# Feeding the first token tiles of a linear-attention kernel by transposing DMAs in place of TensorE transposes

## The chip, the cores and the metric

The kernel runs on one core of a Trainium2 chip. The metric is the device time of one execution in microseconds (us). Before the change it is 194.15 us, the median of three runs (194.1 to 194.21). The profiles are each of one profiled execution of the same program.

## What is computed

Two linear-attention blocks, A and B, read the same input x (2048 tokens, 640 features, bf16), each with its own weights, and a gate mixes them. Cut to what matters:

```python
g = sigmoid((x * gate_w).sum(-1, keepdims=True))
def block(x, wqkv, wo):                 # 32 heads of 20 features
    q, k, v = split(x @ wqkv)
    phi = lambda t: where(t > 0, t + 1, exp(t)) + 1e-6
    kv = einsum("bhsd,bhse->bhde", phi(k), v);  z = phi(k).sum(tokens)
    return ((phi(q) @ kv) / (phi(q) . z + 1e-6)) @ wo
out = g * block(x, A_wqkv, A_wo) + (1 - g) * block(x, B_wqkv, B_wo)
```

## The kernel before

The 2048 tokens are 16 tiles of 128 (`NT`), the 640 features are 5 chunks of 128 (`NC`), and four tiles make a block of 512 tokens (`NB` is 4). In on-chip memory, `XN` holds x with tokens on the partitions and `XT` holds x turned, with features on the partitions. `WKA` and `WKB` hold the K weights, `WQA` and `WQB` the Q weights.

The work runs in stages. First comes K: for each tile, phi(K) = phi(x Wk) is made for A and for B. For one tile this is five pairs of matmuls, one pair for each chunk (512 and 128 columns), which add up in two PSUM banks; then ScalarE takes the exponential and VectorE does two passes. Four PSUM pairs go round. The order of the K stage is A tiles 0 to 3, B tiles 0 to 3, A tiles 4 to 7, B tiles 4 to 7, and so on. Then come Q with the products of x and phi(K), the output weights and denominators, and the output tiles.

K needs the turned x. For tiles 4 to 15 it comes from 15 transposing DMAs (lines 388 to 397), one for each block of four tiles and each chunk, so each turns 512 rows by 128 columns. For tiles 0 to 3, TensorE turns it: `load_xn` brings each tile in by a plain DMA, and `turn` (line 423) multiplies the five chunks by an identity into two PSUM banks (line 431); VectorE copies three chunks and ScalarE two chunks from there into `XT` (lines 445 and 443). For these four tiles K is written out by hand with `ks` (line 824), which calls `k_part` (line 450) for single pairs of tile and chunk; a pair waits only for its own chunk of x and of the weights. All later tiles go through `k_tile` (line 467), whose matmuls wait for all five chunks of the tile. `fill` (line 416) issues matmuls on constants into a bank that is not read.

Every instruction, also the issue of a DMA, goes on the queue of the engine that is named, in the order of the program, and an engine works through its queue in order. An operation waits on semaphores for the last writers of what it reads and for the readers of what it overwrites. SP does nothing but issue DMAs. Its queue before the change is, in order: four plain loads of x (tiles 0 to 3, 160 KB each), chunk 4 of A's K weights, B's K weights (800 KB), the gate column, the 15 transposing DMAs, A's Q weights, three plain loads of x (tiles 4 to 15, 640 KB each), constants, and three more 800 KB weights. ACT's queue begins with chunks 0 to 3 of A's K weights, 160 KB each. The gate column (`gw`, lines 380 to 387) is read by the second group of matmuls of each B tile in `k_tile`.

Of the kernel before, what the change touches and what calls it, by code (L numbers as in the profile page):

```python
# [8 lines left out]
ACT = mybir.ActivationFunctionType  # L9
# [8 lines left out]
NC = 5  # L18
# [187 lines left out]
def bass_gated_mix__linear_attn_block__linear_attn_block__prompt_kernel(  # L206
# [18 lines left out]
    with ExitStack() as es:  # L225
        E = es.enter_context

        def sb(name, shape, dtype=dt.bfloat16):
            return E(nc.sbuf_tensor(name, shape, dtype))
# [5 lines left out]
        XT = sb("XT", [128, NC, S])  # L235
# [33 lines left out]
        def bank(i, lo, hi, p0=0, p1=128):  # L269
            o = 512 * (i % 2)  # L270
            return PP[i // 2][p0:p1, o + lo : o + hi]
# [4 lines left out]
        def new_sem(name):  # L276
            n_sem[0] += 1
            return E(nc.semaphore(name="d%d_%s" % (n_sem[0], name)))
# [3 lines left out]
        def dma(eng, name, o_ap, i_ap, reads=(), writes=(), transpose=False, noncontig=None):  # L282
            sem = new_sem(name)

            def fn(engobj):
                if noncontig is not None:
                    with nc.allow_non_contiguous_dma(reason=noncontig):
                        ins = engobj.dma_start(o_ap, i_ap, transpose=transpose)
                else:
                    ins = engobj.dma_start(o_ap, i_ap, transpose=transpose)  # L290
                return ins.then_inc(sem, 16)

            return sch.op(eng, fn, reads=reads, writes=writes, name=name, sem=sem, total=16)

        def mms(steps, reads=(), writes=(), name=""):


            def fn(pe):
                ins = None
                for o, l, r, st, sp, tp in steps:  # L300
                    ins = pe.matmul(o, l, r, start=st, stop=sp, tile_position=tp)  # L301
                return ins

            return sch.op("PE", fn, reads=reads, writes=writes, name=name)
# [5 lines left out]
        def act(fn, reads=(), writes=(), name=""):  # L310
            return sch.op("ACT", fn, reads=reads, writes=writes, name=name)

        def dve(fn, reads=(), writes=(), name=""):
            return sch.op("DVE", fn, reads=reads, writes=writes, name=name)
# [4 lines left out]
        xin = A_x[0]  # L319


        def load_xn(eng, t0, t1):
            dma(
                eng,
                "xn%d" % t0,
                XN[:, t0:t1, :],
                xin[128 * t0 : 128 * t1, :].rearrange("(t p) f -> p t f", p=128),
                writes=[("XN", t) for t in range(t0, t1)],
            )

        def load_w(eng, name, dst, src, key):
            dma(eng, name, dst[:, :, 0:D], src.rearrange("(c p) f -> p c f", p=128), writes=[key])
# [15 lines left out]
        def load_wk(eng, X, c0, c1):  # L348
            dma(
                eng,  # L350
                "wk%s%d" % (X, c0),
                WK[X][:, c0:c1, 0:D],
                wqkv[X][128 * c0 : 128 * c1, D : 2 * D].rearrange("(c p) f -> p c f", p=128),
                writes=[("WK", X, c) for c in range(c0, c1)],
            )
# [10 lines left out]
                fill=0.0,  # L366
            ),
            reads=[("ONE",)],
            writes=[("IDN",)],
# [2 lines left out]
            lambda e: e.activation(SG[:, 2, 0:1], nc.const_aps.tensor(1.0, (128, 1), dt.float32), ACT.Exp),  # L372
            writes=[("SGE", 0)],
        )
        for t in range(4):
            load_xn("SP", t, t + 1)
            load_wk("ACT", "A", t, t + 1)
        load_wk("SP", "A", 4, NC)
        load_wk("SP", "B", 0, NC)
        dma(  # L380
            "SP",
            "gw",
# [2 lines left out]
            writes=[("GW",)],  # L385
            noncontig="one column",
        )
        for b in range(1, NB):
            for c in range(NC):
                dma(  # L390
                    "SP",
                    "xt%d_%d" % (b, c),
                    XT[:, c, 512 * b : 512 * b + 512],
                    xin[512 * b : 512 * b + 512, 128 * c : 128 * c + 128],
                    writes=[("XT", t, c) for t in range(4 * b, 4 * b + 4)],
                    transpose=True,
                )
        load_w("SP", "wqA", WQ["A"], wqkv["A"][:, 0:D], ("WQ", "A"))
        for b in range(1, NB):
            load_xn("SP", 4 * b, 4 * b + 4)  # L400
        dma("SP", "cst", CB[:, :], cap, writes=[("CST",)])
# [14 lines left out]
        def fill(bk, n, w=512):  # L416
            mms(
                [(bank(bk, 0, w), C1[:, 0:128], C1[:, 0:w], True, True, None)] * n,
                writes=[("PS", bk)],
                name="fill",  # L420
            )

        def turn(t, b0):
            for cs, bk in (((0, 1, 2), b0), ((3, 4), b0 + 1)):
                n = len(cs)
                dst = bank(bk, 0, 64 * n).bitcast(dt.bfloat16)

                def tr(pe, dst=dst, cs=cs):
                    ins = None
                    for i, c in enumerate(cs):  # L430
                        ins = pe.transpose(  # L431
                            dst[:, 128 * i : 128 * i + 128],
                            XN[:, t, 128 * c : 128 * c + 128],
                            IDN[:, :],
                        )
                    return ins

                sch.op("PE", tr, reads=[("XN", t), ("IDN",)], writes=[("PS", bk)], name="tr%d" % t)
                o = XT[:, cs[0] : cs[0] + n, 128 * t : 128 * t + 128]
                i = dst.rearrange("p (c s) -> p c s", c=n)  # L440
                ks = [("XT", t, c) for c in cs]
                if n == 2:
                    act(lambda e, o=o, i=i: e.activation(o, i, ACT.Copy), reads=[("PS", bk)], writes=ks)
                else:
                    dve(lambda e, o=o, i=i: e.tensor_copy(o, i), reads=[("PS", bk)], writes=ks)  # L445
# [4 lines left out]
        def k_part(X, t, pp, cs, first, last):  # L450
            P = PP[pp]
            xs = slice(128 * t, 128 * t + 128)
            bks = [("PS", 2 * pp), ("PS", 2 * pp + 1)]
            for c in cs:
                l = XT[:, c, xs]
                st, sp = first and c == cs[0], last and c == cs[-1]
                mms(
                    [
                        (P[:, 0:512], l, WK[X][:, c, 0:512], st, sp, None),
                        (P[:, 512:D], l, WK[X][:, c, 512:D], st, sp, None),  # L460
                    ],
                    reads=[("XT", t, c), ("WK", X, c)],
                    writes=bks,
                    name="k%s%d" % (X, t),
                )
# [355 lines left out]
                )  # L821


        def ks(*units):
            for t, c in units:
                k_part("A", t, t, (c,), c == 0, c == NC - 1)

        fill(4, 12, 256)
        turn(0, 6)
        fill(4, 1)  # L830
        ks((0, 0))
        turn(1, 6)
        ks((0, 1), (1, 0), (1, 1))
        turn(2, 6)
        ks((0, 2), (1, 2), (2, 0), (2, 1), (2, 2))
        turn(3, 6)
        ks((0, 3), (0, 4))
        ks((1, 3), (1, 4), (2, 3), (2, 4))
        ks(*[(3, c) for c in range(NC)])
        for t in range(4):  # L840
            k_tile("A", t, True)
        for b in range(NB):
            for X in BR:
# [114 lines left out]
```

## Time and profile before

| What | Value |
|---|---|
| Median of the runs | 194.15 us |
| Span of the profiled execution, first to last instruction | 191.9 us |
| Median less span | 2.25 us |
| TensorE (PE) busy | 188.2 us, 98% |
| VectorE (DVE), ScalarE (ACT), GpSimd (POOL) busy | 124.3, 75.0, 44.5 us |
| Start of B tile 0's K on PE | 11.01 us |
| Start of A tile 4's K on PE | 16.47 us |
| Start of Q on PE | 49.11 us |

Times of single events are counted from the first instruction. In the timeline, a row is a run of like instructions: start, length, engine, line of the code, operation, and what is written from what; a "q" behind the engine means that its queue only issues (a DMA). The length of an issue is the time that the queue was held by it. "To landing" is the time from the start of the issue until the data and its semaphore were there. The chain of waits follows the work that ended last back in time, naming at each step what released it. [...]

### The profile page before, as it was taken

Reading aid. Unit: us, or ns where it says so; the run is one execution under the profiler, and the core shown is the slowest. Engines: PE = TensorE matmul, PEld = TensorE weight load, DVE = VectorE, ACT = ScalarE, POOL = GpSimd, SP = SyncE. Lnnn points to the kernel's source line nnn. Section 1 sums busy time; section 2 is a strip of 40 time slices with the busy share of each in tenths; the row PEclk is TensorE's granted clock in tenths of the full one; section 3 lists DMA queues with packets and bytes.
Section 4 is the critical chain, followed back from the end, with each engine's and each line's share of the span. In section 5 each row is a group of like instructions: output and inputs, shape, how many; then the busy total and the mean of one; then the engine's idle time right before and its main releaser. Section 6 shows DMA issues by size and latency. Waiting matters only on the chain.

```text
span 191.9 us, 3569 instructions
## 1 busy us (share of the span) xinstructions
PE 188.2 (98%) x1428; PEld 103.6 (54%) x1428; DVE 124.3 (65%) x211; ACT 75.0 (39%) x130; POOL 44.5 (23%) x36
## 2 busy tenths in 40 slices
PE   7999999999999999999999999999999999999994
PEld 4555555555454444445454557555557555555553
DVE  0298999998996765757676744890422856582544
ACT  3466565565642624444335332122123533223310
POOL 1000223253226566536547410000000000000000
PEclk9999999999999999999999999999999999999999
DMA  5967569993400000011000003038596011111214
GB/s 186 319 119 102 100 104 373 366 352 102 126 3 0 0 3 0 21 43 43 3 0 2 0 25 85 3 67 222 155 254 239 3 68 69 37 68 68 72 38 132
DMA packets 22785, 19.07 MB, mean 99 GB/s; under 512 B 10288, under 2 KB 22000, under 8 KB 22768
## 3 DMA queue, kind: packets, MB, share of 16 engines
q1 hardware_dynamic: 21904, 18.08, 33.4%
q10 hardware_dynamic: 864, 0.76, 1.2%
q8 instruction: 11, 0.18, 0.4%
q14 instruction: 6, 0.05, 0.1%
HBM read 12.94 MB, written 3.93 MB: 88 GB/s over the span
## 4 chain that ended last, share of the span: by engine, by line
PE 96%; DMA 1%; DVE 1%; issue 0%; DVEq 0%
PE ps L301 95%; DMA XN<-in_A_x_dram 1%; PE ps L431 1%; DVE OSTG L796 0%; DVE XT L445 0%; DVEq L928 0%; DVEq L158 0%
## 5 line engine op out<-in xcount | busy, mean ns | idle before, releaser
L525 ACT ACTIVATE EQ<-ps 128x512 bf16<-128x512 f32 x40 | 23.9, 597 | 34.1 <-PE ps L301 34.0
L484 ACT ACTIVATE EK<-ps 128x640 bf16<-128x640 f32 x32 | 22.3, 703 | 16.1 <-PE ps L301 15.2
L530 DVE TENSOR_SCALAR EQ<-EQ 128x512 bf16<-128x512 bf16 x40 | 15.3, 383 | 17.8 <-ACT EQ L525 17.1
L577 POOL TENSOR_TENSOR ZS<-ZS,PKA 128x640 f32<-128x640 f32 x13 | 18.7, 1439 | 27.3 <-DVE PKB L500 12.1
L796 DVE SCALAR_TENSOR_TENSOR OSTG<-ps,SG,PKB 128x640 bf16<-128x640 f32 (+3 forms) x18 | 14.3, 808 | 16.3 <-PE ps L301 16.3
L301 PE MATMUL ps<-PKA,XN 128*128 128x512 bf16 (+1 forms) x160 | 24.8, 299 | 0.0
L301 PE MATMUL ps<-WPA,PQA 128*128 128x512 bf16 (+1 forms) x160 | 24.2, 299 | 0.0
L301 PE MATMUL ps<-WPB,PQB 128*128 128x512 bf16 (+4 forms) x165 | 23.9, 295 | 0.0
L301 PE MATMUL ps<-WKA,XT 128*128 128x512 bf16 (+1 forms) x160 | 23.1, 299 | 0.2
L301 PE MATMUL ps<-XT,WQB 128*128 128x512 bf16 x100 | 23.2, 379 | 0.0
L301 PE MATMUL ps<-XT,WQA 128*128 128x512 bf16 x100 | 23.0, 379 | 0.0
L301 PE MATMUL ps<-WKB,XT 128*128 128x512 bf16 (+1 forms) x160 | 22.5, 299 | 0.0
L779 ACT ACTIVATE PKB<-ps,SG 128x640 f32<-128x640 f32 x16 | 12.7, 795 | 24.9 <-PE ps L301 24.9
L301 PE MATMUL ps<-PKB,XN 128*128 128x512 bf16 (+1 forms) x160 | 22.2, 299 | 0.0
L577 POOL TENSOR_TENSOR ZS<-ZS,PKB 128x640 f32<-128x640 f32 x13 | 19.1, 1469 | 13.5 <-DVE PQB L535 11.0
L301 PEld LDWEIGHTS ps<-PKA,XN 128*128 128x128 bf16 x160 | 13.1, 98 | 11.7
L301 PEld LDWEIGHTS ps<-WPB,PQB 128*128 128x128 bf16 x165 | 13.4, 98 | 8.9
L301 PEld LDWEIGHTS ps<-WPA,PQA 128*128 128x128 bf16 x160 | 12.9, 98 | 9.7
L301 PEld LDWEIGHTS ps<-WKB,XT 128*128 128x128 bf16 x160 | 12.4, 97 | 9.6
L301 PEld LDWEIGHTS ps<-WKA,XT 128*128 128x128 bf16 x160 | 12.3, 98 | 9.7 <-DVE XT L445 0.9
L301 PEld LDWEIGHTS ps<-PKB,XN 128*128 128x128 bf16 x160 | 12.2, 98 | 9.6 <-issue 0.4
L495 DVE TENSOR_SCALAR EK<-EK 128x640 bf16<-128x640 bf16 x32 | 14.6, 456 | 2.6 <-ACT EK L484 2.4
(61 smaller groups left out, 154.2 us busy)
## 6 DMA issues: line engine op xcount, KB each, us to landing
out_dram<-OSTG SPq DMA_DIRECT2D x15, 160.0 KB, 1.8
XN<-in_A_x_dram SPq DMA_DIRECT2D x3, 640.0 KB, 8.8
PKA<-rsA SPq DMA_DIRECT2D x3, 384.0 KB, 4.8
XT<-rsB SPq DMA_DIRECT2D x3, 384.0 KB, 7.3
WKB<-in_B_wqkv_dram SPq DMA_DIRECT2D x1, 800.0 KB, 6.7
WQA<-in_A_wqkv_dram SPq DMA_DIRECT2D x1, 800.0 KB, 5.4
WVA<-in_A_wqkv_dram SPq DMA_DIRECT2D x1, 800.0 KB, 10.6
WQB<-in_B_wqkv_dram SPq DMA_DIRECT2D x1, 800.0 KB, 12.2
```

The source lines that it names most:

```text
L301: ins = pe.matmul(o, l, r, start=st, stop=sp, tile_position=tp)
L431: ins = pe.transpose(dst[:, 128 * i : 128 * i + 128], XN[:, t, 128 * c : 128 * c + 128], IDN[:, :],)
L484: lambda e: e.activation(EK[:, slot, :], P[:, 0:D], ACT.Exp),
L495: lambda e: e.tensor_scalar(EK[:, slot, :], EK[:, slot, :], 1.0, EPS, op0=ALU.min, op1=ALU.add),
L525: lambda e: e.activation(EQ[:, slot, :], bank(bk, 0, 512), ACT.Exp),
L530: lambda e: e.tensor_scalar(EQ[:, slot, :], EQ[:, slot, :], 1.0, EPS, op0=ALU.min, op1=ALU.add),
L577: lambda e: e.tensor_tensor(out=o, in0=a, in1=PK[X][:, t, :], op=ALU.add),
L779: lambda e: e.activation(TA[:, t % 5, :], PP[pp][:, 0:D], ACT.Copy, scale=SG[:, 0, t : t + 1]),
L796: lambda e, lo=lo, hi=hi, p=p: e.scalar_tensor_tensor(out=OSTG[:, slot, lo:hi], in0=p, scalar=SG[:, 1, t : t + 1], in1=TA[:, t % 5, lo:hi] ...
```

## The change

Tiles 1 and 2 are now turned by five transposing DMAs of 256 rows by 128 columns, one for each chunk, and tile 3 by five of 128 rows by 128 columns. These ten open SP's queue, ahead of the gate column and of the 15 of before. Only tile 0 is still turned on TensorE. A's five K weight chunks, the plain load of tile 0 and B's K weights are now issued on ACT's queue, in this order; the plain load of tiles 1 to 3 moves behind A's Q weights on SP's queue. The first four tiles of K for A go in another order: chunk by chunk over tiles 1 and 2, then the turn of tile 0, chunk 0 of tile 3, tile 0, and the rest of tile 3. `first` gives the PSUM pair of each (tile 1 the first, then 2, 0, 3). The fill is 13 matmuls of 256 columns at the start, in place of 12 and a later one of 512 columns.

```diff
-        for t in range(4):
-            load_xn("SP", t, t + 1)
-            load_wk("ACT", "A", t, t + 1)
-        load_wk("SP", "A", 4, NC)
-        load_wk("SP", "B", 0, NC)
+        def load_xt(t0, t1, c):
+            dma(
+                "SP",
+                "xt%d_%d" % (t0, c),
+                XT[:, c, 128 * t0 : 128 * t1],
+                xin[128 * t0 : 128 * t1, 128 * c : 128 * c + 128],
+                writes=[("XT", t, c) for t in range(t0, t1)],
+                transpose=True,
+            )
+
+        for c in range(NC):
+            load_xt(1, 3, c)
+            load_wk("ACT", "A", c, c + 1)
+        load_xn("ACT", 0, 1)
+        load_wk("ACT", "B", 0, NC)
+        for c in range(NC):
+            load_xt(3, 4, c)
...
         for b in range(1, NB):
             for c in range(NC):
...
+                load_xt(4 * b, 4 * b + 4, c)
         load_w("SP", "wqA", WQ["A"], wqkv["A"][:, 0:D], ("WQ", "A"))
+        load_xn("SP", 1, 4)
...
+        first = (1, 2, 0, 3)
+
         def ks(*units):
             for t, c in units:
-                k_part("A", t, t, (c,), c == 0, c == NC - 1)
-
-        fill(4, 12, 256)
-        turn(0, 6)
-        fill(4, 1)
-        ks((0, 0))
-        turn(1, 6)
-        ks((0, 1), (1, 0), (1, 1))
-        turn(2, 6)
-        ks((0, 2), (1, 2), (2, 0), (2, 1), (2, 2))
-        turn(3, 6)
-        ks((0, 3), (0, 4))
-        ks((1, 3), (1, 4), (2, 3), (2, 4))
-        ks(*[(3, c) for c in range(NC)])
-        for t in range(4):
+                k_part("A", t, first.index(t), (c,), c == 0, c == NC - 1)
+
+        fill(4, 13, 256)
+        for c in range(NC):
+            ks((1, c), (2, c))
+        turn(0, 4)
+        ks((3, 0))
+        ks(*[(0, c) for c in range(NC)])
+        ks(*[(3, c) for c in range(1, NC)])
+        for t in first:
             k_tile("A", t, True)
```

More of the change, by code (lines that the diff above doesn't have):

```diff
@@ L389, in bass_gated_mix__linear_attn_block__linear_attn_block__prompt_kernel @@
             for c in range(NC):
[L390 to L397, printed above, removed]
+                load_xt(4 * b, 4 * b + 4, c)
         load_w("SP", "wqA", WQ["A"], wqkv["A"][:, 0:D], ("WQ", "A"))
+        load_xn("SP", 1, 4)
         for b in range(1, NB):
```

## The prediction

> **What bounds the kernel now.** I read the chain of waits on the profile's page first.
>
> ```profile
> PE 96%; DMA 1%; DVE 1%; issue 0%; DVEq 0%
> PE ps L301 95%; DMA XN<-in_A_x_dram 1%; PE ps L431 1%; DVE OSTG L796 0%; DVE XT L445 0%; DVEq L928 0%; DVEq L158 0%
> ```
>
> TensorE bounds the span: line 301 is every matmul but the transposes. So a change at the start counts by how far it moves the matmuls behind it. Next, the same chain in order of time (start, length, what), from 0 to 20 us.
>
> ```profile
> 0.80 2.77 DMA XN<-in_A_x_dram
> ...
> 4.04 0.37 DVE XT L445
> ...
> 5.10 0.37 DVE XT L445
> ...
> 8.19 12.02 PE ps L301 x86
> ```
>
> Until 3.57 us the chain is the first load of x; then two copies out of PSUM stand in it, 0.37 us each; from 8.19 on it is matmuls alone. All that the change can win lies before about 8 us. Third, the timeline of PE, with the starts that I compare against.
>
> ```profile
> 0.84 2.72 PE L301 MATMUL ps<-const-bfloat16-1.0 128*128 128x256 bf16 x12 [0.84 <-PEq L943]
> ...
> 8.03 3.15 PE L301 MATMUL ps<-WKA,XT 128*128 128x512 bf16 x22
> 11.01 5.61 PE L301 MATMUL ps<-WKB,XT 128*128 128x512 bf16 x40
> 16.47 5.59 PE L301 MATMUL ps<-WKA,XT 128*128 128x512 bf16 x40
> ```
>
> B tile 0 starts at 11.01 and A tile 4 at 16.47, so a tile costs (16.47 - 11.01) / 4 = 1.365 us, and a unit (one tile, one chunk) a fifth, 0.273 us. Four tiles of A are 20 units, 5.5 us; between 3.62 (first transpose) and 11.01 lie 7.4 us. The other 1.9 us are 20 transposes and waits for copies.
>
> Fourth, SP's queue: the answer on tile XT between 8.8 and 26 us, and from the timeline and the DMA issues the transpose issued at 11.39 us, chunk 4 of tiles 4 to 7.
>
> ```profile
> L290 SPq DMA_TRANSPOSE XT<-in_A_x_dram x13: 1262/1262/1555, 8.8 to 24.7; - x13
> DMA to landing us min/median/max: 2.8/3.6/4.8
> ```
>
> ```profile
> 11.39 1.26 SPq L290 DMA_TRANSPOSE XT<-in_A_x_dram  x1
> ```
>
> ```profile
> XT<-in_A_x_dram SPq DMA_TRANSPOSE x1, 4.8
> ```
>
> Two things are to be seen. A 512-row transpose holds SP for 1.26 us whatever the DMA load, and the next starts 0.04 us later (24.7 after 8.8 us is twelve steps of 1.3): the queue, not the transfer, sets the pace. And chunk 4 of tiles 4 to 7 lands at 11.39 + 4.8 = 16.2 us, while PE asks for it at 16.47. **The margin is 0.25 us.** Behind the issue's end, the landing takes 2.8 - 1.26 = 1.5 us at least, 2.3 in the median, 3.5 at most.
>
> **The change part by part.**
>
> *Ten more transposes on SP, ahead of those 15.* No 256- or 128-row transpose is in the trace; the nearest rows are the 512-row one (1.26 us) and a plain load of 128 rows of x or weights, which holds SP or ACT for 0.40 to 0.46 us, as does an 800 KB load of 640 rows (0.43). Lower bound: cost in proportion to rows, 0.63 and 0.32 us. Upper bound: independent of rows, 1.26. I take a fixed part equal to a plain issue, 0.43, and the rest by rows: 0.43 + 0.83 x rows/512, so 0.85 for 256 rows and 0.64 for 128. The plain issues hardly depend on their rows, so a queue instruction that costs nothing fixed is not what the trace shows. Nothing makes it a gain: the queue is in order.
>
> *SP's queue after it.* It starts at 0.80 as now. Five at 0.85 + 0.04: to 5.2. Five at 0.64 + 0.04: to 8.6. The gate column, 0.53 + 0.04: to 9.2. Five of 512 rows at 1.30: to 15.7. Before, the fifth's issue ended at 12.65, because only plain loads stood ahead (4.19), although the first two were held up to 2.05 and 2.46 us behind 800 KB of weights in the same queue. That hold-up goes, since the weights move to ACT: a credit of 2.0 us that is already in the sum. Chunk 4 of tiles 4 to 7 lands at 15.7 + 2.3 = **18.0**.
>
> [...]
>
> *PE until then.* Fills: 13 in place of 12 of 256 columns at about 0.22 us (2.72 / 12), over at about 3.8; they cover the wait for the first data. The first transpose's issue ends at 1.65; the run's first DMA landed 2.77 - 0.40 = 2.4 us behind its issue, so chunk 0 comes at about 4.0. Then chunks come every 0.89 us and feed two units of 0.55: PE waits for DMA until chunk 4 lands at 5.2 + 2.3 = 7.5, and ends these ten units at 8.05. Turn of tile 0: five transposes and a copy, 0.28 + 0.40, with unit (3, 0) under the copy: 8.75. Tile 0: 1.36, to 10.1. The rest of tile 3 would end at 11.2; its last chunk is issued at 8.6 and lands at 10.9, so 11.2 stands. **B tile 0 starts at about 11.2 against 11.01**: the three turns taken away (15 transposes, two copy waits) are paid back by waiting for chunks. If ACT's 1.76 MB of weights and x, sharing the DMA engines until about 8 us, delay the chunks by another microsecond, this is 12.2. Bounds: 10.2 (proportional issue, below) to 16.4 (issue independent of rows: tile 3's last chunk issued at 13.8, landing at 16.1).
>
> *B tiles 0 to 3.* 4 x 1.365: to 16.65. Their weights, on ACT, are issued by about 4 and have 7 us (6.7 to landing now). The gate column, issued at 9.2, lands by 11.5, needed behind the first five matmuls of B tile 0, at 12.3. PSUM: A tile 1, ready at 8.05, frees its pair some 2 us later by the rows of exponential and two passes (0.70 + 0.32 + 0.82), before B tile 0. Both cost nothing.
>
> *A tile 4: the wait.* PE arrives at 16.65 and chunk 4 lands at 18.0. So A tile 4 starts at **18.0 against 16.47: +1.5 us**. Queued behind that wait is all the rest of PE's program, and on ACT and DVE the K passes. A second microsecond of delay in the first tiles would vanish under it.
>
> *Behind it.* Tiles 8 to 11: their last issue ends at 15.7 + 6.5 = 22.2, landing 24.5; PE arrives at 18.0 + 10.9 = 28.9. Hidden. A's Q weights are issued 2.7 us later (26.04 to 28.7), and 480 KB of x is added to the stream; at the 370 GB/s of the stretch from 30 to 36 us that is 1.3 us. Q starts at 49.11, and these weights landed at 31.4: 17 us of cover. If it were gone, Q would wait in full. Nothing of 1.5 us is given back, as PE's waits behind it sum to 0.4 us in the view of waits.
>
> *Sum.* Span 191.9 + 1.5 = 193.4. The median stands 2.25 above the span (194.15), so 195.65; I say **195.6**.
>
> **The rivals.**
>
> *Proportional issue, faster.* Ten transposes cost 0.67 and 0.36 with their gaps: SP reaches the gate column at 5.9, and block 1 is issued by 13.0 and lands at 15.3. Then PE decides: chunk 4 of tiles 1 and 2 at 4.15 + 2.3 = 6.45, units done 7.0, turn and copy 7.7, tile 0 at 9.05, tile 3 at 10.15, B to 15.6: -0.9, or 193.3. For it: the issue of 512 rows is so much longer than a plain one that rows must count. Against: plain issues show a floor of 0.40. It decides if the fixed part is under about 0.2 us. [...]
>
> *Near balance.* Fixed part 0.35 and the shortest landing, 1.5: chunk 4 of block 1 (tiles 4 to 7) lands at 16.7: +0.2, 194.4.
>
> *Flat issue.* Each transpose costs 1.30 with its gap: ten to 13.8, gate 14.4, block 1 to 20.9, landing 23.2: +6.7, or 200.9. For it: 13 rows of one size cannot exclude it.
>
> **How the numbers follow.** Forecast 0.66, proportional 0.18, balance 0.08, flat 0.08. With these traces about 0.2% (0.4 us) can be told from no change. From the forecast's case 0.03 falls within it, from the proportional one 0.01, and all of the balance: faster 0.17, same 0.12, slower 0.71. The low end, 193.3, reaches to the proportional case; the high end, 198.0, takes a fixed part of 0.8 us (block 1 at 20.3) and leaves the flat case out. The forecast's own range is 194.5 to 197.
>
> **What would show it.** Right: the new transposes hold SP for about 0.85 and 0.64; block 1's first issue at 9.2; an idle stretch of PE ahead of A tile 4, put down to the DMA of XT; B tile 0 near 11. Wrong: issues of 0.6 and 0.3, or A tile 4 with no wait. It would also fail if transposes and plain loads, in flight together, slowed one another by microseconds: the trace of before has them one behind the other.

## The result and the profile after

The changed kernel takes 202.3 us in the median of five runs (201.36 to 203.15), beside 194.1 us for the kernel before on the same chip (194.03 to 194.21). The ratio is 1.0414, 95% interval 1.0388 to 1.0440: 8.2 us slower, where 1.5 us were forecast. The time lies outside the range of 193.3 to 198.0. The profiled execution is the slowest of the five: 203.15 us with a span of 201.4, so 9.5 us more span than before.

The chain of waits on the page of the changed kernel, by engine and by line:

```profile
PE 90%; DMA 5%; SPq 2%; issue 1%; ACT 1%; DVE 0%; DVEq 0%
PE ps L301 90%; DMA XT<-in_A_x_dram 5%; SPq L290 2%; ACT WPB L750 1%; DVE OSTG L802 0%; PE ps L437 0%; DVEq L932 0%; DVEq L158 0%
```

TensorE's share fell from 96% to 90%; the transposing DMAs and their issue have come in with 5% and 2%. In order of time, the same chain shows where:

```profile
3.35 1.25 SPq L290
4.59 0.04 issue
4.63 9.09 DMA XT<-in_A_x_dram
13.73 0.05 issue
13.77 2.31 PE ps L301 x8
```

One transposing DMA, issued at 4.63 us, took 9.09 us to land: chunk 3 of tiles 1 and 2. PE's timeline (start, length, and in brackets the idle time before and what ended it):

```profile
4.26 1.25 PE L301 MATMUL ps<-WKA,XT 128*128 128x512 bf16 x4 [0.50 <-DMA XT<-in_A_x_dram]
6.82 0.72 PE L301 MATMUL ps<-WKA,XT 128*128 128x512 bf16 x4 [1.31 <-DMA XT<-in_A_x_dram]
9.19 1.25 PE L301 MATMUL ps<-WKA,XT 128*128 128x512 bf16 x4 [1.65 <-DMA XT<-in_A_x_dram]
13.77 2.31 PE L301 MATMUL ps<-WKA,XT 128*128 128x512 bf16 x8 [3.34 <-DMA XT<-in_A_x_dram]
...
20.52 5.61 PE L301 MATMUL ps<-WKB,XT 128*128 128x512 bf16 x40
25.97 5.60 PE L301 MATMUL ps<-WKA,XT 128*128 128x512 bf16 x39
```

B tile 0 starts at 20.52 in place of 11.01. That is 9.5 us, the whole loss of the span. A tile 4 follows 5.45 us behind, as before (16.47 - 11.01 = 5.46): the wait that was forecast there does not occur. (Starts are compared, as the rows of matmuls overlap: in the kernel before, a matmul of 512 columns in the row at 11.01 us lasts 379 ns, and the next starts 216 ns behind its start.) So the first four tiles of K are all that is to be explained. The transposes issued up to 13.65 us, and the stretches 3.8 to 9.0 and 13.7 to 18.6 us (busy time of PE, PEld, DVE, ACT, POOL, granted clock, DMA share, GB/s):

```profile
L290 SPq DMA_TRANSPOSE XT<-in_A_x_dram x10: 1222/1232/1320, 0.8 to 12.4; - x10
DMA to landing us min/median/max: 2.9/5.4/9.1
```

```profile
3.80:9.00 5.20, 1.96 (x8) 0.66 (x8) 0.00 (x0) 0.00 (x0) 0.00 (x0) 0.98 1.02 189
13.70:18.60 4.90, 4.80 (x20) 2.34 (x21) 1.25 (x3) 1.57 (x3) 0.00 (x0) 0.50 0.39 71
```

And the first stretch of the kernel before, from 4 to 9 us:

```profile
4.00:9.00 5.00, 4.81 (x44) 2.76 (x41) 1.43 (x4) 1.76 (x5) 0.00 (x0) 1.00 1.08 348
```

Three things can be seen. The new transposes of 256 and of 128 rows hold SP for 1.23 us in the median, hardly less than those of 512 (1.26). The DMA engines are as busy as before, about 1.0 and 1.1, but move 189 GB/s in place of 348. And TensorE's granted clock is 0.50 from 13.7 to 18.6; the trace has it at 0.50 from 8.8 to 19.0.

The packets in the traces of these two stretches (3.8 to 9.0 and 4 to 9 us) say where the yield goes. Most packets of the plain loads (1280 bytes) take as long as before, with a median of 56 ns against 55, but the mean is 110 ns against 58.6: 73 of 662 last over 150 ns, the longest 2.2 us, and they are almost half of the plain loads' busy time. The packets of the transposes (256 bytes) take 20 ns on average and make only 0.13 of the share of 1.02. So the yield is lost in a few packets of plain loads that take far longer than the rest, and not by the small size of the transposes' packets.

### The profile page after: what moved, and what is told of

Read it like the earlier page. It is cut to its first block, busy times and chain, and to the rows that moved or that the text cites. A ratio compares the mean times of both kernels' runs of the same rounds, so it can differ in the third digit from the quotient of the medians.

```text
span 201.4 us, 3522 instructions
## 1 busy us (share of the span) xinstructions
PE 189.5 (94%) x1387; PEld 104.0 (52%) x1413; DVE 123.7 (61%) x208; ACT 73.9 (37%) x127; POOL 44.5 (22%) x36
## 4 chain that ended last, share of the span: by engine, by line
PE 90%; DMA 5%; SPq 2%; issue 1%; ACT 1%; DVE 0%; DVEq 0%
PE ps L301 90%; DMA XT<-in_A_x_dram 5%; SPq L290 2%; ACT WPB L750 1%; DVE OSTG L802 0%; PE ps L437 0%; DVEq L932 0%; DVEq L158 0%
## 5 line engine op out<-in xcount | busy, mean ns | idle before, releaser
L301 PE MATMUL ps<-WKA,XT 128*128 128x512 bf16 (+1 forms) x157 | 26.4, 325 | 7.0 <-DMA XT<-in_A_x_dram 6.8
L536 DVE TENSOR_SCALAR EQ<-EQ 128x512 bf16<-128x512 bf16 x40 | 15.3, 383 | 17.8 <-ACT EQ L531 17.1
L583 POOL TENSOR_TENSOR ZS<-ZS,PKA 128x640 f32<-128x640 f32 x13 | 18.7, 1439 | 27.3 <-DVE PKB L506 12.1
L802 DVE SCALAR_TENSOR_TENSOR OSTG<-ps,SG,PKB 128x640 bf16<-128x640 f32 (+3 forms) x18 | 14.3, 808 | 16.3 <-PE ps L301 16.3
L301 PE MATMUL ps<-WPA,PQA 128*128 128x128 bf16 (+1 forms) x155 | 23.3, 297 | 0.4 <-ACT WPB L750 0.2
L301 PE MATMUL ps<-WPB,PQB 128*128 128x128 bf16 (+4 forms) x162 | 23.2, 294 | 0.2
L301 PEld LDWEIGHTS ps<-WKA,XT 128*128 128x128 bf16 x160 | 13.2, 104 | 19.4 <-DMA XT<-in_A_x_dram 8.8
L301 PE MATMUL ps<-XT,WQB 128*128 128x512 bf16 x99 | 23.2, 379 | 0.1
L301 PE MATMUL ps<-WKB,XT 128*128 128x129 bf16 (+1 forms) x157 | 22.3, 297 | 0.2
L301 PE MATMUL ps<-PKB,XN 128*128 128x512 bf16 (+1 forms) x156 | 21.7, 297 | 0.3 <-issue 0.2
L301 PEld LDWEIGHTS ps<-WPA,PQA 128*128 128x128 bf16 x160 | 12.9, 98 | 9.7
L301 PEld LDWEIGHTS ps<-WKB,XT 128*128 128x128 bf16 x160 | 12.4, 97 | 9.6
```

The costliest lines, as they stand in the source:

```text
L536: lambda e: e.tensor_scalar(EQ[:, slot, :], EQ[:, slot, :], 1.0, EPS, op0=ALU.min, op1=ALU.add),
L583: lambda e: e.tensor_tensor(out=o, in0=a, in1=PK[X][:, t, :], op=ALU.add),
L802: lambda e, lo=lo, hi=hi, p=p: e.scalar_tensor_tensor(out=OSTG[:, slot, lo:hi], in0=p, scalar=SG[:, 1, t : t + 1], in1=TA[:, t % 5, lo:hi] ...
```

## The experiments

Three theories were set against each other. Theory F: a transposing DMA holds SP's queue for about 1.23 us whatever its rows, and this alone decides. Theory M: transposes and plain loads that are in flight together slow one another. Theory C: idle stretches halve TensorE's clock, which costs on its own. Times of events below are those of each run's profiled execution. Ratios are to the kernel before on the same chip.

### One part alone: the K weights on ACT's queue

```diff
-        load_wk("SP", "A", 4, NC)
-        load_wk("SP", "B", 0, NC)
+        load_wk("ACT", "A", 4, NC)
+        load_wk("ACT", "B", 0, NC)
```

> The kernel before with one part of the change alone: A's last K weight chunk and B's K weights go to ACT's queue; no new transposes. SP's queue then reaches the 15 transposes near 3.2 us in place of 4.2, and they are in flight beside B's K weights. Theory M: those weights land at 12 us or later in place of 9.8, B tile 0 waits for them, 195.5 to 197 us. Theory F: the transposes only come earlier, B tile 0 starts at 11.0 and the time is 194.1 us, as before.

Measured: 197.22 us, ratio 1.0171 (1.0112 to 1.0229), just above the 195.5 to 197 of theory M. B's K weights, from the DMA issues; the start of B tile 0; and VectorE's pass that the profile names as its releaser:

```profile
WKB<-in_B_wqkv_dram ACTq DMA_DIRECT2D x1, 800.0 KB, 10.8
```

```profile
14.13 5.61 PE L301 MATMUL ps<-WKB,XT 128*128 128x512 bf16 x40 [1.80 <-DVE PKA L500]
```

```profile
11.02 0.82 DVE L500 SCALAR_TENSOR_TENSOR PKA<-ps,EK 128x640 bf16<-128x640 f32 x1
```

The weights were issued at 3.2 us, so they landed at 14.0; before, it was 3.14 + 6.7 = 9.8. B tile 0 starts right behind, at 14.13. The bracket names VectorE, but the pass that frees its PSUM pair ended at 11.84, 2.3 us before that start; the weights landed 0.1 us before it, so it waited for them. No transpose was added; the 15 old ones only came into flight beside plain loads of the other queue. Theory M said this, F did not. It is a loss and not only another order of service: by 10.0 us the packets of this run had moved 1643 KB of plain loads and 128 KB of transposes, those of the kernel before 2240 and 173.

### A plain load beside the transposes, and behind them in their queue

B's Q weights, needed only much later, are moved from the end of SP's queue to ACT's, behind tile 3's exponential:

```diff
         for t in range(4):
             k_tile("A", t, True)
+        load_w("ACT", "wqB", WQ["B"], wqkv["B"][:, 0:D], ("WQ", "B"))
```

> The kernel before with one plain load moved: B's Q weights (800 KB, needed only in the Q stage) leave the end of SP's queue and are issued on ACT's queue behind the K exponentials of tile 3, near 13 us, in the midst of the 15 transposes. Theory M: that load lands 8 us or more behind its issue, and the transposes issued beside it land 5 us or more behind their start (2.8 to 4.8 before); the time is between 194 and 196 us, since tiles 8 to 11 have some 4 us of cover. Theory F: it lands in about 5.5 us, as A's Q weights do alone (5.4), the transposes keep 2.8 to 4.8, 194.2 us.

Measured: 196.47 us, 1.0100 (1.0034 to 1.0167); the four runs spread from 194.3 to 198.3. The load and the transpose issued beside it (chunk 4 of tiles 4 to 7), and A tile 4:

```profile
WQB<-in_B_wqkv_dram ACTq DMA_DIRECT2D x1, 800.0 KB, 5.1
XT<-in_A_x_dram SPq DMA_TRANSPOSE x1, 6.9
```

```profile
18.65 5.59 PE L301 MATMUL ps<-WKA,XT 128*128 128x512 bf16 x40 [1.89 <-DMA XT<-in_A_x_dram]
```

The partner, the same load on SP's queue behind the transposes of tiles 4 to 7:

```diff
+            if b == 1:
+                load_w("SP", "wqB", WQ["B"], wqkv["B"][:, 0:D], ("WQ", "B"))
```

> The partner of the run before it: the same 800 KB at about the same time, but on SP's own queue, behind the five transposes of tiles 4 to 7. Theory M (only loads of another queue mix; in one queue one follows the other): it lands in about 5 us, the transposes behind it are 2 to 3 us later and then as quick as before, 194.2 us. If any plain load near transposes were slow, whatever its queue, it would land in 8 us or more here too.

Measured: 193.99 us, 1.0008 (0.9996 to 1.0019).

```profile
WQB<-in_B_wqkv_dram SPq DMA_DIRECT2D x1, 800.0 KB, 5.9
```

Half of what I expected of theory M fell. The load on ACT was not slow (5.1 us, not 8 or more), and quicker than its partner (5.9). It is the transpose that lost: 6.9 us to landing, landed at 18.4 against 15.5 in the partner (issued at 11.99, 3.54 to landing), and it cost 2 us at A tile 4.

The pair does not show that the other queue is the reason. ACT issued the load at 11.43, earlier than the 13 us expected and 0.12 us ahead of that transpose (11.55); in the partner it was issued at 13.29, behind it. From the issue of the load to the landing of the next transpose issued after it, it is 7.0 us here (11.43 to 18.41) and 6.4 in the partner (13.29 to 19.73). So in both queues the transpose came behind the load that was issued first, and only here the delayed one was chunk 4, for which TensorE waits.

### B's K weights behind the new transposes

```diff
-        load_wk("ACT", "B", 0, NC)
         for c in range(NC):
             load_xt(3, 4, c)
+        load_wk("SP", "B", 0, NC)
```

> The change, but B's K weights (800 KB) leave ACT's queue and stand on SP behind tile 3's transposes, so that only 960 KB of plain loads are in flight beside the transposes. Theory M (plain loads of ACT's queue and transposes of SP's queue, in flight together, slow one another): chunk 3 of tiles 1 and 2, issued near 4.6 us, lands by about 9 us in place of 13.7, chunk 4 by about 10; B tile 0 then waits for its weights, issued at 13.6, until 17 to 18, so 199 to 200 us against 202.3. Theory F (only the issue time counts, 1.23 us for each transpose whatever its rows, and the late landings are a backlog of SP's own queue): chunk 3 stays near 13.7 and the time is 202 us or more.

Measured: 203.13 us, 1.0442 (1.0376 to 1.0509). The ten transposes:

```profile
L290 SPq DMA_TRANSPOSE XT<-in_A_x_dram x10: 1222/1232/1242, 0.8 to 12.3; - x10
DMA to landing us min/median/max: 2.3/2.5/4.7
```

Chunk 3 of tiles 1 and 2 among them, issued at 4.63 us, and B tile 0 with what comes before it:

```profile
XT<-in_A_x_dram SPq DMA_TRANSPOSE x1, 3.6
```

```profile
11.84 3.47 PE L301 MATMUL ps<-WKA,XT 128*128 128x512 bf16 x20
18.87 7.29 PE L301 MATMUL ps<-WKB,XT 128*128 128x512 bf16 x40 [3.56 <-DMA WKB<-in_B_wqkv_dram]
```

Chunk 3 took 3.6 us to land in place of 9.1, so it was there at 8.3, not 13.7: the backlog was not one of SP's own queue. Theory M was right on this landing. The first four tiles are done at 15.3. But the 199 to 200 us that it gave were missed, and no time was won: the weights, behind ten issues of 1.23 us, land at 18.7, 3.6 us later than TensorE wants them, and TensorE then runs B in part at half pace (7.29 us for 40 matmuls against 5.61; the granted clock is 0.50 from 19.7 to 23.1).

### Five transposes in place of ten

```diff
-            load_xt(1, 3, c)
+            load_xt(1, 4, c)
...
-        for c in range(NC):
-            load_xt(3, 4, c)
```

> The change, but tiles 1 to 3 are turned by five transposes of 384 rows in place of five of 256 and five of 128. Both theories: each holds SP for about 1.25 us, and the first transpose of tiles 4 to 7 is issued near 7.7 us in place of 14.3. Theory F (issue time alone): chunk 4 lands near 9, B tile 0 starts near 13.5 and the time is about 195.5 us. Theory M (mixing with 1.76 MB of plain loads): chunks 3 and 4 still land at 12 us or later, B tile 0 starts at 17 or later, 199 us or more.

Measured: 202.43 us, 1.0415 (1.0373 to 1.0457).

```profile
12.98 2.31 PE L301 MATMUL ps<-WKA,XT 128*128 128x512 bf16 x8 [2.36 <-DMA XT<-in_A_x_dram]
...
18.83 5.61 PE L301 MATMUL ps<-WKB,XT 128*128 128x512 bf16 x40
```

SP reached the transposes of tiles 4 to 7 at 7.9 us in place of 14.3, and nothing was won: chunk 3, issued at 4.67, still landed only at 12.9. The 195.5 us of theory F were missed by 7: issue time alone is not the cause.

### Both repairs together

```diff
-            load_xt(1, 3, c)
+            load_xt(1, 4, c)
...
-        load_wk("ACT", "B", 0, NC)
-        for c in range(NC):
-            load_xt(3, 4, c)
+        load_wk("SP", "B", 0, NC)
```

> Two repairs of the change at once: tiles 1 to 3 by five transposes of 384 rows, and B's K weights on SP's queue behind them, so that 960 KB of plain loads are beside the transposes. If the loss is issue time and mixing together, each hiding the other in the runs that took away one: the five issues end near 7.2, chunk 4 lands by 10, B's K weights by 12, B tile 0 starts near 14 and A tile 4 near 19.5, about 197 us. If something else holds the first tiles (the half clock, or the transposes' own transfer), B tile 0 starts at 17 or later and the time stays near 202.

Measured: 198.53 us, 1.0243 (1.0213 to 1.0274).

```profile
8.34 3.83 PE L301 MATMUL ps<-WKA,XT 128*128 128x512 bf16 x16 [3.13 <-DMA XT<-in_A_x_dram]
...
15.45 5.61 PE L301 MATMUL ps<-WKB,XT 128*128 128x512 bf16 x40
20.90 5.60 PE L301 MATMUL ps<-WKA,XT 128*128 128x512 bf16 x40
```

Each repair alone gained nothing; both bring the ratio from 1.0414 to 1.0243, some 3.3 us. With one cause taken away, the other still holds B tile 0 back to 18.8 or 18.9 us: late chunks in the run with five transposes, late weights in the one before it. Chunk 4 landed at 10.0 (5.96 + 4.04), as expected; B tile 0 came 1.5 us later than expected, because the eight units behind chunk 1 went at 0.46 us each (12.00 - 8.34 over 8) in place of 0.27; the granted clock is 0.59 on average from 8.3 to 12.0.

### The clock

```diff
             ks((1, c), (2, c))
+            fill(6, (8, 8, 14, 0, 0)[c])
```

> The change with 8, 8 and 14 more matmuls on constants (512 columns, into a bank not yet in use) behind the units of chunks 0, 1 and 2 of tiles 1 and 2, where TensorE idles for data. Theory C (the half clock between about 9 and 19 us comes from the idle stretches and costs time of its own): the granted clock stays at 1.00, the 14 units and the turn behind chunk 3 take about 4.5 us in place of 6.8, B tile 0 starts near 18.3, and the time is about 200 us. Its rival (the clock follows something else, or its loss is hidden under the DMA waits): clock 0.5 as before, or 202 us in spite of a full clock.

Measured: 201.66 us, 1.0380 (1.0350 to 1.0410). The clock reads 1.00 in all four runs, but the trace of the profiled one has no clock record at all, and a view without a record prints 1.00. The pace of the matmuls shows the full clock: the eight behind chunk 3 take 1.26 us, in place of 2.31.

```profile
14.00 1.26 PE L301 MATMUL ps<-WKA,XT 128*128 128x512 bf16 x8 [0.63 <-DMA XT<-in_A_x_dram]
...
18.55 5.61 PE L301 MATMUL ps<-WKB,XT 128*128 128x512 bf16 x40
```

From chunk 3 to B tile 0 it is 4.55 us in place of 6.75, so between these two executions the clock is worth 2.2 us. They are the fastest of this run's four and the slowest of the changed kernel's five. The median moves by 0.6 only, and the intervals overlap. So theory C holds in the profile, where with the gaps filled the eight matmuls took 1.26 us and not 2.31; in the time it is not shown, as 201.66 lies nearer to the rival's 202 than to the 200 of theory C.

### All loads on one queue

In the run with five transposes, the seven plain loads of ACT go ahead of them on SP:

```diff
+        for c in range(NC):
+            load_wk("SP", "A", c, c + 1)
+        load_xn("SP", 0, 1)
+        load_wk("SP", "B", 0, NC)
         for c in range(NC):
             load_xt(1, 4, c)
```

> The second run (tiles 1 to 3 by five transposes of 384 rows) with the seven plain loads of ACT's queue put on SP's queue, ahead of the five transposes: same transfers, one queue. Theory M: no mixing, so the weights land by about 7.5 us, each transpose lands within 2.5 us of its issue's end, chunk 4 at 13 to 14 us although it is issued 3 us later, and the time is 198 to 200 us against 202.4. Theory F: all of SP's queue is 3 us later than there and so is everything else, 204 us or more.

Measured: 202.31 us, 1.0432 (1.0408 to 1.0456). A miss for both.

```profile
11.18 4.50 PE L301 MATMUL ps<-WKA,XT 128*128 128x512 bf16 x20 [7.41 <-DMA XT<-in_A_x_dram]
```

Chunk 4 landed at 12.8 (9.45 + 3.37), near the 13 to 14 of theory M, and A's K weights at 6.0. But B's landed at 10.7 and no transpose before 11.1, so TensorE stood idle for 7.4 us and then ran at half pace (granted clock 0.50) until 14.5 us. In this one queue the transposes did not overtake, and the plain loads with transposes behind them were still slower than the 7.5 us expected. So "another queue" is not the whole of the mixing.

### Transposes of 1536 rows

The kernel before, with the 15 transposes of 512 rows as five of 1536:

```diff
-        for b in range(1, NB):
-            for c in range(NC):
...
-                    XT[:, c, 512 * b : 512 * b + 512],
-                    xin[512 * b : 512 * b + 512, 128 * c : 128 * c + 128],
+        for c in range(NC):
...
+                XT[:, c, 512:S],
+                xin[512:S, 128 * c : 128 * c + 128],
```

> The kernel before with tiles 4 to 15 turned by five transposes of 1536 rows in place of fifteen of 512. If the issue is flat in rows also above 512, each holds SP for 1.3 to 1.8 us (the transfer's own pace, 96 packets of 18 ns on each engine, is 1.7), the fifth ends near 15 and lands near 17, A tile 4 waits about 0.5 us: 194.2 to 195. If the rows count above 512 (3.8 us each), the fifth lands near 25 and the time is about 203 us.

Measured: 199.99 us, 1.0309 (1.0274 to 1.0344).

```profile
L290 SPq DMA_TRANSPOSE XT<-in_A_x_dram x5: 1469/2004/5492, 4.2 to 16.7; - x5
DMA to landing us min/median/max: 4.1/6.0/8.2
```

```profile
21.11 7.27 PE L301 MATMUL ps<-WKA,XT 128*128 128x512 bf16 x40 [4.34 <-DMA XT<-in_A_x_dram]
```

The issue that was not held up is 1.47 us: from 128 rows (1.23 us in the changed kernel) to 1536, twelve times as many, it grows by a fifth. The transfer is then what paces: the five landings are 12.4, 14.5, 17.4, 19.3 and 20.9, on average 2.1 us apart. A tile 4 needs all five and starts 4.6 us late, and then runs at half pace for 3.4 us (7.27 us for 40 matmuls against 5.59). Both forecasts of the time, 194.2 to 195 and 203, were missed: the issue is flat, as the first said, but the first transpose landed only at 12.4, behind B's K weights (10.1), and the others followed 2.1 us apart, not 1.7.

### The order on TensorE

Both repairs, and tile 0 first:

```diff
+        turn(0, 6)
+        fill(4, 2)
+        for c in range(NC):
+            ks((0, c), (1, c), (2, c), (3, c))
```

The plain load of tile 0 opens ACT's queue here, and `first` is (0, 1, 2, 3).

> The run before it with the work on TensorE put in the order in which its data can come: the plain load of tile 0 opens ACT's queue, tile 0 is turned right behind the fill, and each chunk's units go over tiles 0 to 3. If the data alone sets the end of the first four tiles, B tile 0 starts near 11 to 12, and A tile 4 waits for its transposes (issued by 15, landing at 17 to 18): 194.8 to 196 us, still no gain over 194.1, because the queue of SP is then what is late. If it comes out below 193.8, the change's idea was sound and only its place in the queues was not.

Measured: 196.05 us, 1.0107 (1.0089 to 1.0125).

```profile
7.92 4.25 PE L301 MATMUL ps<-WKA,XT 128*128 128x512 bf16 x30 [1.09 <-DMA XT<-in_A_x_dram]
13.37 5.62 PE L301 MATMUL ps<-WKB,XT 128*128 128x512 bf16 x40 [1.20 <-DVE PKA L505]
18.83 5.60 PE L301 MATMUL ps<-WKA,XT 128*128 128x512 bf16 x40
```

This is the best form of the change that was tried, still 2 us slower. Chunk 1 lands at 7.9, and 15 of the 20 units are still to do then, 4.1 us; so the first four tiles end no earlier than 12.0, against 11.0 before. All four end together, and the exponential and two passes of the first hold B tile 0 for another 1.2 us. The wait at A tile 4 that was expected does not occur (its transposes land by 16.5, it starts at 18.83), so the time came out next to the expected 194.8 to 196 by another path. No run was faster than the kernel before, and none points to a version that would be.

## Why the prediction was wrong, point by point

**What bounds the kernel** was right: only the start moved. From B tile 0 on, all of it is shifted, by 20.52 - 11.01 = 9.5 us, as the span is.

**The step that failed first** is the cost of an issue, "0.43 + 0.83 x rows/512". I took 0.85 and 0.64 us; they are 1.24 and 1.23 in the median. The truth lay next to my upper bound, 1.26 "independent of rows", and I gave the flat rival a chance of 0.08. The trace of before held the hint: plain issues of 128 and of 640 rows cost the same, 0.43. I used these rows for the fixed part and not for the slope. As a result SP was through with the ten at 13.6 (forecast 8.6, flat rival 13.8), and chunk 4 of tiles 4 to 7 landed at 22.2 (18.0 and 23.2). The flat rival had the queue right. That its time, 200.9, is also near is in part luck, as it came from a wait at A tile 4 that did not occur. The same holds for the direction: I forecast slower, but by that wait. And "1.26 us whatever the DMA load" was read too widely: the row itself has 1.555 at most, two issues of the kernel before were held for 2.05 and 2.46, and in the run with five transposes one was held for 3.17.

**The step that failed most** is the first tiles: "if ACT's 1.76 MB ... delay the chunks by another microsecond", which was to vanish under the wait at A tile 4. Even with flat issue, chunk 3 would have landed at 4.63 + 1.24 + 2.3 = 8.2; it landed at 13.7, with B's K weights at 13.2. The delay was 5.5 us, and it came at a place with nothing behind to hide it. B's K weights, for which I allowed 7 us, took 9.2. The forecast's last sentence had named transposes and plain loads in flight together as what could break it, but without a price or a chance: a rival that I saw and did not work out. Most of it was B's K weights: with them off ACT's queue, chunk 3 was there at 8.3.

**The clock** was no term of the sum. It cost some 2.2 us in the profiled execution; what it costs in the median is not shown.

**The sum, as the runs give it.** With B's K weights out of the way the first tiles end at 15.3, 4.3 us behind 11.0. By an estimate, flat issue alone keeps that end at 14.9 or later: the last of the ten transposes lands at 14.65, and one unit of 0.27 needs it; what mixing is left and a half pace up to 12.8 us (0.53 us for a unit from 8.13 on) stand beside it. With those weights beside the transposes, but TensorE kept busy, B tile 0 starts at 18.55: 3.3 more. With the clock as it falls, 20.52: 2.0 more. Together 9.5, for the profiled execution; the median loses 8.2. The parts depend on each other, as the two repairs showed, so this is one order of taking them away, not a law.

**What held:** the credit for the hold-up that goes (the first transposes of tiles 4 to 7 held SP for 1.19 and 1.27 us, in place of 2.05 and 2.46), and the cover behind (A's Q weights landed at 40.4, Q began at 58.6). The wait at A tile 4 was not there, only because TensorE came later still than 22.2.

## What to carry to other kernels

Price a queue by the number of its instructions before their size: where an issue is nearly all fixed cost, as here (1.23 us at 128 rows, 1.26 at 512), ten small transfers cost the queue as much as ten large ones. When two kinds of transfer have only been seen one behind the other, their running side by side is an unknown with a price of its own (here 5.5 us at chunk 3); bound it by microseconds, not by shares. A repair that gains nothing alone is not refuted until its partner has been tried with it.

## What the runs showed of the hardware

In the changed kernel a transposing DMA held SP's queue for 1.23 us at 128 rows and for 1.22 to 1.32 at 256. At 512 rows it was 1.26 in most cases (kernel before), at 1536 it was 1.47 in the shortest of five.

With the new transposes beside plain loads, from 3.8 to 9.0 us, the DMA engines moved 189 GB/s at a busy share of 1.02; in the kernel before, from 4 to 9 us, it was 348 at 1.08. In the changed kernel chunk 2 landed 0.2 us behind tile 0's plain load (9.14 and 8.93), chunk 3 0.5 us behind B's K weights (13.73 and 13.24). How the engines share their time inside was not shown, and stays open; so does why plain loads were slowed with several in flight (10.8 us for 800 KB) and hardly with one (5.1).

A granted clock of 1.00 in the profile can mean that no record is there. In the run with five transposes it reads 1.00 throughout, yet the eight matmuls at 12.98 us take 2.31 us, as in the changed kernel at a granted 0.50. The first clock record of that trace is at 16.27 us, and up to there the matmuls run at half pace: a matmul of 512 columns takes 427 ns from its start to the next one's, against 216 later on. In the changed kernel the first record is at 5.38 us, in the kernel before at 3.74, and the fills ahead of them run at half pace too (213 ns for 256 columns, about what 512 columns take later). The pace of like matmuls is the surer sign.

The granted clock of the changed kernel fell to 0.50 at 8.79 us, in a gap of 1.65 us behind others of 0.50 and 1.31. In the 3.41 us since it had risen, at 5.38, TensorE was busy for 0.85. In the run with a plain load on ACT the 40 matmuls behind a gap of 1.89 us between busy stretches kept the full pace (5.59 us). So here the clock fell after several shorter gaps in a row, and after that single longer one the pace did not fall.
